# More engines for two early kinds of work, and an instruction order searched anew: attention in hash buckets with a two-layer network behind it

## The chip, the cores and the metric

The kernel runs on one core of one Trainium2 chip. TensorE (PE, with PEld for its weight loads) does the matrix products, VectorE (DVE), ScalarE (ACT) and GpSimd (POOL) the elementwise work, SyncE (SP) issues the transfers. Each engine works through its own instructions in the order in which they were written, and they wait for each other by semaphores. The metric is the time of one execution on the device in microseconds (us); less is better. Three executions of the kernel before took 867.09, 869.69 and 871.51 us.

## The reference

```python
# q, k, v: (4, 8, 768, 64), times 0.1; proj: (64, 6); w_in: (512, 2048); w_out: (2048, 512)
q_bits = (einsum('bhsd,dk->bhsk', q, proj) > 0);  k_bits = (einsum('bhsd,dk->bhsk', k, proj) > 0)
mask = bucket(q_bits)[:, :, :, None] == bucket(k_bits)[:, :, None, :]      # the six bits as a number
scores = where(mask, matmul(q, k^T) / sqrt(64), -1e9)
attn = exp(scores - max(scores));  attn = attn / (sum(attn) + 1e-9)
x = matmul(attn, v), its heads side by side: (3072, 512)
out = (maximum(x @ w_in, 0) ** 2) @ w_out                                   # (3072, 512)
```

## The kernel before

Work goes by visits: one batch, one pair of heads, one third of the 768 queries. Each visit has four units of 128 queries by 768 keys. A unit's scores go to a PSUM tile (`pS`, later also `side`), VectorE takes the row maxima (`line`), ScalarE the exponentials with their sums (`e`, `sm`), and `rv` becomes one over the sum. The attention is then transposed (`aT`) and multiplied by the values (`pA`); four visits give one block of 256 tokens, and `moe` runs the two layers on it (`pm` against `win`, `po` against `wo`), interleaved with the next visits.

The matrix products of most stages are made of float16 pairs, a high and a low part. Only the first visits are "plain": their scores are products in float32 with the mask's rows set into the same operands (`A`, `L`, `Q`, `M`; some rows of these are made on VectorE and ScalarE out of the PSUM tile `side`), and for the first four of them the division `e * rv` is written back to `e`, and TensorE transposes it against the unit matrix `unit_f` into `pT`. A visit that isn't plain divides into the pair `hl`, which a transfer transposes.

The weights come as 64-bit integers holding a double each. `fetch` loads a piece of 128 x 512 shifted by two bytes (`raw`, in `room`), has one 16-bit half of each number copied out ("the top half", `move(first...)`), and VectorE then joins it with the rest. There are 32 such pieces, 16 of each matrix; a norm of each group (`sq`, `norm`) and the split into a high and a low part follow.

Nothing of the order is written by hand. `Program` collects all operations with their dependences. Some name several engines that may do them ("ways"). A planner in the kernel's own code then lists them: `forward` takes, at each moment of its own clock, the ready operation of best priority on each engine, and chooses among ways by estimated end; `backward` and 24 `rounds` set the priorities; then each number in `PATH` stands for one pseudo-random shake of the priorities (`shake`), all kept, one after the other. The last `forward` is the order emitted. Estimated times decide on engines and order alone: on the chip every wait is a real semaphore.

Transfers are estimated so, one after another at `HBM` = 265 bytes a ns (265 GB/s), with a shorter time for those issued in the first `SOON_TO` ns:

```python
done *= SOON if t < SOON_TO else 1.0                       # forward and replay; SOON, SOON_TO = 0.7, 22000
dma = max(dma, t + busy + (650 if k != "pool" else 450))   # when this transfer may start
dma += done
done = dma + 910 - t                                       # when its data has landed
```

`emit` also fills TensorE's queue: where the plan has TensorE idle before the first transposition, it puts products of the constant `ones` (tile `idle`), in number after the planned gap:

```python
fill[i] = int((o.start - end) * IDLE_SHARE / 56) if fill else int((o.start - end) * 0.95 / 107)
```

with `IDLE_SHARE` = 0.6. The functions that the change touches:

Of the kernel before, what the change touches and what calls it, by code (L numbers as in the profile page):

```python
# [13 lines left out]
BF16 = mybir.dt.bfloat16  # L14
# [35 lines left out]

ROUNDS, BEHIND = 24, 40000
PATH = (
# [13 lines left out]
)  # L66
LOADS = 0

# [3 lines left out]

PLAIN, PLAIN_TO, ALTERNATE, DOUBLE = 4, 12, 16, 34

PLAIN_AV, DIVIDE = (0, 1, 2, 3), ("pool",)

AV_RUN = 18

# [15 lines left out]

SWITCH, ENTRY = 95, 105
TRANSPOSES, HBM, SMALL = 165, 265, 300
SOON, SOON_TO = 0.7, 22000


class Buffer:  # L100
# [477 lines left out]
def lsh_attention_moe(ctx: ExitStack, tc, kq, v, proj2, w_in, w_out, consts, out):  # L578
# [5 lines left out]
    pe, dve, act, pool, sp = pr.pe, pr.dve, pr.act, pr.pool, pr.sp  # L584
# [3 lines left out]
    def send(out, x):  # L588
        sp.dma_start(out, x)

    def move(out, x, scale=1.0, engines=(act, dve, pool)):
        ways = [(q, "tensor_scalar", (out, x, scale, 1.0, ALU.mult, ALU.mult), {}) for q in engines if q not in (act, sp)]
        if act in engines:
            ways.append((act, "activation", (out, x, AF.Identity if isinstance(scale, View) else AF.Copy), {"scale": scale}))
        if sp in engines:
            ways.append((sp, "dma_start", (out if out.dtype == x.dtype else out.bitcast(x.dtype), x), {}))
        pr.add(*ways)
# [67 lines left out]
    def fetch(src):  # L665

        raw = place(turn[0] % 2 * 4096, 4096, U32).rearrange("p (n t) -> p n t", t=2)
        send(raw.rearrange("p n t -> p (n t)").bitcast(U16)[:, 0:2047], src.bitcast(U16)[:, 1:2048])
        first = tops[turn[0] % len(tops)]
        turn[0] += 1  # L670
        move(first[:, :, 1], raw.rearrange("p n t -> p (n t)").bitcast(BF16).rearrange("p (n t) -> p n t", t=4)[:, :, 2], 1.0, (dve, pool))
        f = place(12288 + turned[0] % ((ROOM - 12288) // 2048) * 2048, 2048, F32)
        turned[0] += 1
        dve.scalar_tensor_tensor(f.bitcast(U32), raw[:, :, 0], 13, first.rearrange("p n t -> p (n t)").bitcast(U32), ALU.logical_shift_right, ALU.bitwise_or)
        return f
# [16 lines left out]
    def split(srcs, parts, name):  # L692

        fs = [fetch(src) for src in srcs]
        pt = small("pt")
        for n, f in enumerate(fs):
            sq = sb([P, 512], BF16, "sq", 2)
            square(sq, f)
            pe.matmul(pt, ones, sq, start=n == 0, stop=n == len(fs) - 1)
        norm = sb([P, 1], F32, "norm")  # L700
        dve.tensor_reduce(norm, pt, AX.X, ALU.max)
        to, back = scales(norm, name, 4)
        for f, (hi, lo) in zip(fs, parts):
            move(hi, f, to)
            left(lo, f, to, hi)
        return to, back
# [405 lines left out]
```

## Time and profile before

| | before |
|---|---|
| median of three executions | 869.69 us (867.09 to 871.51) |
| the profiled execution | 867.13 us |
| its span, first to last instruction | 865.1 us, 16,996 instructions |
| mean granted TensorE clock over the span | 0.996 of full speed |
| busy: TensorE, ScalarE, VectorE, GpSimd | 832.1, 666.0, 661.7, 111.5 us |

All rows and views are of the one profiled execution, so 867.13 - 865.1 = 2.03 us of its time lie outside the span. A matmul's row ends by a model and matmuls are pipelined, so busy time of TensorE includes short waits in its pipeline. Most operations are recorded by one helper line, L565, and are told apart by their tiles.

### The profile page before, as it was taken

Reading aid. Unit: us, or ns where it says so; the run is one execution under the profiler, and the core shown is the slowest. Engines: PE = TensorE matmul, PEld = TensorE weight load, DVE = VectorE, ACT = ScalarE, POOL = GpSimd, SP = SyncE. Lnnn points to the kernel's source line nnn. Section 1 sums busy time; section 2 is a strip of 40 time slices with the busy share of each in tenths; the row PEclk is TensorE's granted clock in tenths of the full one; section 3 lists DMA queues with packets and bytes.
Section 4 is the critical chain, followed back from the end, with each engine's and each line's share of the span. In section 5 each row is a group of like instructions: output and inputs, shape, how many; then the busy total and the mean of one; then the engine's idle time right before and its main releaser. Section 6 shows DMA issues by size and latency. Waiting matters only on the chain.

```text
span 865.1 us, 16996 instructions
## 1 busy us (share of the span) xinstructions
PE 832.1 (96%) x6340; PEld 543.8 (63%) x6343; DVE 661.7 (76%) x1448; ACT 666.0 (77%) x1153; POOL 111.5 (13%) x175
## 2 busy tenths in 40 slices
PE   6999978998999999999999999999999999999997
PEld 4555555665566667667666667676666666766664
DVE  4889988999696999877796888885887988871111
ACT  3897867699796888877886898977887888883332
POOL 0554464310010100000000001000100000000000
PEclk8999999999999999999999999999999999999999
DMA  8426979865788898787575978797665798771000
GB/s 298 128 82 185 195 197 226 188 117 108 177 168 189 159 166 163 143 156 169 134 156 153 165 155 146 151 159 164 135 111 157 145 150 150 135 147 38 1 25 25
DMA packets 301634, 125.77 MB, mean 145 GB/s; under 512 B 279792, under 2 KB 287728, under 8 KB 301552
## 3 DMA queue, kind: packets, MB, share of 16 engines
q1 hardware_dynamic: 301264, 124.61, 68.6%
q8 instruction: 50, 0.82, 0.4%
q14 instruction: 32, 0.26, 0.1%
q10 hardware_dynamic: 288, 0.08, 0.0%
HBM read 37.36 MB, written 6.29 MB: 50 GB/s over the span
## 4 chain that ended last, share of the span: by engine, by line
PE 73%; DVE 11%; ACT 8%; issue 3%; DMA 3%; POOL 1%; SPq 0%; ACTq 0%; DVEq 0%; POOLq 0%
PE pm L565 24%; PE po L565 24%; PE pA L558 9%; PE pS L565 8%; PE side L565 6%; DVE line L563 3%; ACT e L565 3%; DVE hl L565 2%; ACT g L565 1%; ACT hl L565 1%; PE pd L558 1%; DMA unit_f<-consts 1%; DMA V<-vp 1%; DVE room L565 1%; PE pc L565 1%
## 5 line engine op out<-in xcount | busy, mean ns | idle before, releaser
L565 PE MATMUL pm<-xx,win 128*128 128x256 f16 x2304 | 308.3, 273 | 3.0 <-DVE g L565 1.2
L565 PE MATMUL po<-wo,g 128*128 128x512 f16 x1152 | 298.7, 379 | 4.7 <-ACT acc L565 3.2
L565 PEld LDWEIGHTS <-win 128*128 128x128 f16 x2304 | 223.0, 98 | 84.0 <-issue 18.0
L565 DVE SCALAR_TENSOR_TENSOR hl<-e,rv,hl 128x768 f16<-128x768 f32 x176 | 179.5, 1025 | 15.8 <-ACT hl L565 14.8
L565 PEld LDWEIGHTS <-g 128*128 128x128 f16 x1152 | 111.4, 98 | 107.6 <-issue 11.2
L565 ACT ACTIVATE hl<-e,rv 128x768 f16<-128x768 f32 x168 | 155.2, 928 | 8.3 <-DVE rv L565 3.8
L563 DVE TENSOR_REDUCE line<-pS 128x1 f32<-128x768 f32 x113 | 107.8, 954 | 21.0 <-PE pS L565 18.9
L565 ACT ACTIVATE g<-g 128x512 f32<-128x512 f32 (+1 forms) x184 | 114.7, 625 | 10.3 <-PE po L565 7.7
L565 POOL TENSOR_SCALAR rv<-sm 128x1 f32<-128x1 f32 x98 | 37.9, 387 | 590.5 <-ACT e L565 558.3
L565 DVE SCALAR_TENSOR_TENSOR g<-g,g 128x512 f16<-128x512 f32 x84 | 57.7, 686 | 69.1 <-ACT g L565 69.0
L565 ACT ACTIVATE g<-pm 128x512 f32<-128x512 f32 x93 | 55.0, 591 | 68.6 <-PE pm L565 68.5
L558 PE MATMUL pA<-aT,VV 128*64 128x256 f16 x1584 | 94.9, 274 | 0.0
L558 PEld LDWEIGHTS <-VV 128*64 128x64 f16 x1584 | 83.1, 110 | 12.9 <-issue 12.5
L565 ACT ACTIVATE e<-pS,pair 128x768 f32<-128x768 f32 x72 | 71.0, 986 | 24.0 <-DVE pair L563 13.8
L565 ACT ACTIVATE e<-side,pair 128x768 f32<-128x768 f32 x72 | 71.0, 986 | 12.6 <-DVE pair L563 7.3
L563 DVE TENSOR_REDUCE line<-side 128x1 f32<-128x768 f32 x79 | 75.2, 951 | 5.0 <-PE side L565 4.0
L565 ACT ACTIVATE e<-pS,line 128x768 f32<-128x768 f32 x41 | 36.9, 899 | 8.3 <-DVE line L563 6.8
L565 PEld LDWEIGHTS <-room 128*128 128x128 f16 x288 | 27.8, 98 | 18.3 <-issue 1.3
L565 PE MATMUL pS<-A,L 128*128 128x384 f32 x84 | 34.9, 529 | 4.6 <-DVE L L565 2.4
L565 PE MATMUL pS<-room 128*128 128x384 f16 x144 | 36.0, 326 | 0.0
L565 PE MATMUL side<-room 128*128 128x384 f16 x144 | 34.6, 326 | 0.0
L565 PE MATMUL pS<-Q,M 128*128 128x384 f32 x80 | 31.3, 503 | 2.5 <-ACT e L565 2.3
(164 smaller groups left out, 905.6 us busy)
## 6 DMA issues: line engine op xcount, KB each, us to landing
R<-kq SPq DMA_DIRECT2D x24, 384.0 KB, 4.1
room<-w_in SPq DMA_DIRECT2D x16, 511.8 KB, 3.9
room<-w_out SPq DMA_DIRECT2D x16, 511.8 KB, 3.7
V<-vp SPq DMA_DIRECT2D x16, 384.0 KB, 4.1
out<-acc SPq DMA_DIRECT2D x24, 256.0 KB, 2.8
room<-room SPq DMA_DIRECT2D x60, 96.0 KB, 2.9
aT<-hl SPq DMA_TRANSPOSE x176, 3.9
Q<-kq SPq DMA_DIRECT2D x6, 384.0 KB, 4.1
```

The source lines that it names most:

```text
L558: ins = q.engine.matmul(*map(real, args), **kw).ins
L563: issue(q, getattr(q.engine, name)(*map(real, args), **{k: real(x) for k, x in kw.items()}).ins)
L565: ins = getattr(q.engine, o.name)(*map(real, o.args), **{k: real(x) for k, x in o.kw.items()}).ins
```

## The change

Two calls get more ways, the estimate of the first transfers loses its factor, and `PATH` holds another list: 233 shakes (400004 to 440621) give way to 3,588 (960005 to 1002083).

```diff
 PATH = (
-    400004, 400029, 400036, 400042, 400059, 400060, 400072, 400092, 400101, 400104, 400119, 400137, 400139, 400148, 400157, 400162, 400198, 400206,
...
+    960005, 960006, 960007, 960008, 960010, 960012, 960013, 960014, 960019, 960020, 960021, 960022, 960024, 960025, 960027, 960028, 960030, 960032,
...
-PLAIN_AV, DIVIDE = (0, 1, 2, 3), ("pool",)
+PLAIN_AV, DIVIDE = (0, 1, 2, 3), ("pool", "dve", "act")
...
-SOON, SOON_TO = 0.7, 22000
+SOON, SOON_TO = 1.0, 0
...
-        move(first[:, :, 1], raw.rearrange("p n t -> p (n t)").bitcast(BF16).rearrange("p (n t) -> p n t", t=4)[:, :, 2], 1.0, (dve, pool))
+        move(first[:, :, 1], raw.rearrange("p n t -> p (n t)").bitcast(BF16).rearrange("p (n t) -> p n t", t=4)[:, :, 2], 1.0, (dve, pool, act))
```

`DIVIDE` is used at one place, `move(e, e, rv, ...)` of a plain unit: 16 divisions of 128 x 768 numbers in float32. The call in `fetch` is the copy of the top halves: 32 of them, 128 x 512 numbers of 16 bits. With the new ways ScalarE may do either kind as an activation (a copy, or a multiplication by a value per row), and VectorE the divisions too. Which engine gets which is the planner's choice.

## Rows read from the trace of the kernel before

**Rows 1.** The page: busy time of each engine with its share of the span and its number of instructions.

```profile
PE 832.1 (96%) x6340; PEld 543.8 (63%) x6343; DVE 661.7 (76%) x1448; ACT 666.0 (77%) x1153; POOL 111.5 (13%) x175
```

**Rows 2.** Busy time by stretch (the windows view). Columns: stretch in us from the span's start, its length, busy us of each engine with its number of instructions, granted TensorE clock as a share of full speed, busy share of the DMA engines, GB/s.

```profile
10.00:20.00 10.00, 4.23 (x8) 2.17 (x9) 3.97 (x9) 3.63 (x8) 0.76 (x1) 0.74 0.85 322
20.00:60.00 40.00, 37.21 (x207) 21.17 (x209) 34.36 (x74) 35.79 (x73) 20.22 (x29) 0.98 0.34 109
60.00:110.00 50.00, 47.15 (x286) 27.91 (x285) 47.09 (x99) 39.84 (x75) 23.91 (x28) 1.00 0.81 185
110.00:150.00 40.00, 33.21 (x217) 20.15 (x218) 35.28 (x67) 30.04 (x53) 21.61 (x23) 1.00 0.85 203
150.00:200.00 50.00, 47.62 (x336) 30.08 (x334) 47.92 (x98) 41.60 (x70) 9.93 (x17) 1.00 0.81 167
200.00:600.00 400.00, 394.86 (x3169) 260.83 (x3169) 329.58 (x742) 332.33 (x570) 23.50 (x49) 1.00 0.79 157
600.00:850.00 250.00, 250.00 (x1988) 169.69 (x1988) 156.84 (x344) 175.20 (x300) 10.84 (x22) 1.00 0.54 105
```

**Rows 3.** The chain that ended last, followed through its first 32 us. Columns: start in us, us, what.

```profile
2.63 7.21 DMA V<-vp
...
9.87 7.42 DMA unit_f<-consts
...
17.32 0.23 DVE ident L565
...
18.17 0.56 DVE Q L565
```

**Rows 4.** VectorE's instructions in order of time, 0 to 20 us. Columns: start in us, us, engine, line, operation, out<-in with shapes, count, and in brackets the idle time before it and what ended it.

```profile
17.32 0.23 DVE L565 CAST ident<-unit_f 128x128 bf16<-128x128 f32 x1 [5.70 <-DMA unit_f<-consts]
...
18.76 0.96 DVE L563 TENSOR_REDUCE line<-pS 128x1 f32<-128x768 f32 x1
```

**Rows 5.** TensorE's matmuls in order of time, 0 to 32 us, same columns.

```profile
0.99 4.00 PE L554 MATMUL idle<-ones 128*128 128x128 bf16 x38 [0.99 <-POOL ones L565]
...
7.25 1.45 PE L554 MATMUL idle<-ones 128*128 128x128 bf16 x23
11.14 1.41 PE L565 MATMUL pS<-A,L 128*128 128x384 f32 x2 [2.45 <-DVE L L565]
...
12.67 1.49 PE L565 MATMUL pS<-A,L 128*128 128x384 f32 x2
18.78 0.48 PE L565 MATMUL side<-bits,sgn 128*128 128x384 bf16 x1 [4.62 <-DVE Q L565]
19.05 2.75 PE L565 MATMUL pS<-A,L 128*128 128x384 f32 x4
...
29.60 0.81 PE L565 MATMUL pS<-A,L 128*128 128x384 f32 x2
...
30.89 1.46 PE L565 MATMUL pS<-A,L 128*128 128x384 f32 x4
```

**Rows 6.** All engines in order of time, 0 to 32 us, same columns: the first transfer's issue, and the first users of some of the first transfers.

```profile
0.74 0.40 SPq L565 DMA_DIRECT2D Q<-kq  x1
...
3.81 0.56 DVE L565 TENSOR_SCALAR M<-Q 64x768 f32<-64x768 f32 x1 [1.26 <-DMA Q<-kq]
...
7.92 0.56 DVE L565 TENSOR_SCALAR L<-A 64x768 f32<-64x768 f32 x1 [2.32 <-DMA A<-kq]
...
8.93 0.56 DVE L565 TENSOR_SCALAR M<-Q 64x768 f32<-64x768 f32 x1 [0.46 <-DMA Q<-kq]
...
9.87 0.84 ACT L565 ACTIVATE sqv<-V 128x768 bf16<-128x768 f32 x1 [3.00 <-DMA V<-vp]
...
13.49 0.76 POOL L565 TENSOR_SCALAR room<-room 128x512 f16<-128x512 bf16 x1 [8.40 <-DMA room<-w_in]
```

**Rows 7.** Groups of instructions by form in the stretch 0 to 200 us, GpSimd, then VectorE, then ScalarE. Columns: line, engine, operation, out<-in with shapes and count | busy us, mean ns of one | idle time before them and what ended it.

```profile
L565 POOL TENSOR_SCALAR room<-room 128x512 f16<-128x512 bf16 x26 | 24.8, 963 | 14.2 <-DMA room<-w_in 10.6 <-DMA room<-w_out 2.9
L565 POOL TENSOR_SCALAR e<-e,rv 128x768 f32<-128x768 f32 x16 | 17.0, 1064 | 15.4 <-DVE rv L565 10.0 <-PE side L565 1.7 <-DVE fromwin L565 1.4
...
L565 DVE TENSOR_SCALAR room<-room 128x512 f16<-128x512 bf16 x6 | 2.9, 481 | 0.1
...
L565 DVE TENSOR_SCALAR hl<-e,rv 128x768 f16<-128x768 f32 x2 | 1.2, 612 | 0.0
...
L565 ACT ACTIVATE hl<-e,rv 128x768 f16<-128x768 f32 x25 | 23.2, 928 | 1.2 <-DVE rv L565 1.2
...
L565 ACT ACTIVATE g<-g 128x512 f16<-128x512 f32 x8 | 5.0, 628 | 4.2 <-PE po L565 4.1
```

**Rows 8.** GpSimd's instructions on the tiles e (the divisions) and room (the copies of the top halves, to 200 us), one row each. Columns: line, engine, operation, out<-in, count: shortest, median and longest ns, first and last start in us, form.

```profile
L565 POOL TENSOR_SCALAR e<-e,rv x16: 904/907/1323, 24.4 to 75.2; 128x768 f32<-128x768 f32 x16
...
L565 POOL TENSOR_SCALAR room<-room x26: 757/774/1513, 13.5 to 164.0; 128x512 f16<-128x512 bf16 x26
```

**Rows 9.** What TensorE waited for, 20 to 200 us and then 200 to 600 us. Columns: who waited <- for whom: us in total, times, the longest.

```profile
PE pS L565 <- ACT e L565: 4.2, 6, 1.7
PE side L565 <- DVE Q L565: 2.2, 5, 0.8
PE pT L565 <- ACT aT L565: 1.2, 2, 0.9
...
PE po L565 <- ACT acc L565: 3.2, 5, 0.8
```

212 rows, old and new, of the table PATH are left out of this document.

## The prediction

> **What bounds the kernel now.** Read the busy shares first: TensorE has work in 96% of the span, no other engine in more than 77% [rows 1]. A change to engines off TensorE's queue can so give back no more than the time in which TensorE waits, 865.1 - 832.1 = 33.0 us. The view by stretches says where that is [rows 2]. From 600 to 850 us TensorE is busy 250.00 of 250 us: nothing to win. From 200 to 600 us it is idle 5.1 us. From 20 to 200 us the busy times sum to 165.2 of 180 us, idle 14.8, the worst part being 110 to 150 us with 6.8. From 10 to 20 us it is busy 4.23 of 10 us, and the granted clock is 0.74, a mixture of the two levels of 2.4 and 1.2 GHz; from 60 us on it is 1.00. So the change must earn its time in the first 200 us, where it also acts: the divisions by GpSimd lie between 24.4 and 75.2 us, its copies of top halves between 13.5 and 164.0 us [rows 8].
>
> Next the chain of waits through the start [rows 3]. Two transfers head it: the first `V`, and then `unit_f`, issued at 9.87 and landed 7.42 us later, for a single VectorE cast (`ident`) at 17.32 us. VectorE had been idle 5.70 us ahead of that cast [rows 4], and what is queued behind it was ready long before: a pair of score products had started on TensorE at 11.14 us and run 1.41 us [rows 5], yet the row maximum of the first scores runs at 18.76 us [rows 4]. TensorE's next product, at 18.78 us, waits 4.62 us for the `Q` that VectorE makes at 18.17 us [rows 3, 5]. An in-order queue is thus held by a transfer whose result nothing needs so early.
>
> The stall has a second price. The score products around it run slow: pairs of 1.41 and 1.49 us and a run of four in 2.75 us, together 5.65 us; later a pair takes 0.81 and a run of four 1.46, so the same eight would take 3.08 us [rows 5]. That is 2.6 us at the lower clock after idle time.
>
> **The estimates of first transfers.** The planner's formulas can be held against the landings. For loads of 384 KB (393,216 bytes) one after another, with about 1.9 us ahead of the first (issue from 0.74 [rows 6], then 0.475 and 0.65 by the code) and 0.91 behind, the old estimate has 0.7 x 393,216 / 265 = 1.04 us each, landing at about 3.8, 4.9, 5.9, 7.0 and 8.0 us; the new one 1.48 us each, at 4.3, 5.8, 7.2, 8.7 and 10.2. The first users started at 3.81 (first), 7.92 and 8.93 (third and fourth) and 9.87 (fifth) [rows 6]. The old estimate is up to 2 us early, the new one within 0.7 us. Ahead of `unit_f` lie ten such loads and two of 512 KB, 4.98 MB in all: the old estimate lands it at about 1.9 + 13.2 + 0.2 + 0.9 = 16.2 us, the new one at 21.8, the trace at 17.29 [rows 3]. So the old plan put work behind transfers that came later than it believed; the new plan, if wrong, is wrong on the side where data waits for its user.
>
> **The change part by part.**
>
> *Start.* With the later estimate the planner has a reason to put the cast of `ident` behind the row maxima and the `Q` rows. From above: the whole TensorE wait of 4.6 us and the 2.6 us at the lower clock, 7.2 us. From below 0: the transfers keep the DMA engines 85% busy from 10 to 20 us [rows 2], and another late piece (a `V`, an integer piece of the weights) may stop the same queue. The cast's own wait is the nearest row and most of it has no need to be; against that VectorE is busy 34.4 of the next 40 us and ScalarE 35.8 [rows 2], so part of an earlier start is lost downstream. I take 4.0.
>
> *Filling products.* Longer planned gaps mean more products of `ones` in TensorE's queue. The first gap had 38, in 4.00 us [rows 5]: 105 ns each. The plan's landing of the second load moves by 0.9 us, which at 0.95 / 107 is 8 more, 0.8 us, and real work behind them waits if data is there first. On the other side filled gaps hold the clock up: after 23 of them, from 7.25 us, the next real product came at 11.14 [rows 5]. Bounds -2.6 (already in the 7.2 above) and +0.8; taken: +0.3.
>
> *Copies of top halves.* Now 26 on GpSimd of 963 ns and 6 on VectorE of 481 [rows 7]. ScalarE's price isn't in the trace; the nearest row is its conversion of 128 x 512, 628 ns [rows 7]. Each copy moved from GpSimd shortens one step by about 0.34 us and the longest, 1,513 ns [rows 8], by 0.9. But nobody on the path stands behind them much: GpSimd is busy 75.7 of 180 us from 20 to 200 us.
>
> *Divisions.* Now 16 on GpSimd of 1,064 ns. Nearest rows: the same sizes, but with a 16-bit result, on VectorE 612 ns and on ScalarE 928 [rows 7]. A division moved is 0.14 to 0.45 us shorter, on the path from the exponential to the transposition. Yet TensorE's waits at the transpositions name ScalarE's `aT` (1.2 us) [rows 9], the copy after them. Both kinds together: gain 0 to 2, taken 0.5. What hides their new cost is ScalarE's idle time: 180 - 147.3 = 32.7 us from 20 to 200 us [rows 2]. All 42 from GpSimd would cost 26 x 0.628 + 16 x 0.928 = 31.2 us, all of that cover; about a third of them, 10 us, fits. The waits 20 to 200 us show what happens without cover: the largest, 4.2 us, are on ScalarE's exponentials [rows 9], which would stand behind a copy in the same queue.
>
> GpSimd's shortest copy takes 757 ns, its longest 1,513, and the division 904 to 1,323 [rows 8]: something holds it at times. The Trainium skill (SBUF — State Buffer, section "SBUF: two separate sides") says that VectorE and GpSimd share one pair of ports, which one of them locks for a whole instruction; the spread agrees with it. It also speaks against the new way on VectorE: a VectorE division would lock out GpSimd. By that rule alone the sum would lose, at 0.612 us each for 16, at most 9.8 us of GpSimd's time, which is idle for more than half of this stretch, and so nothing at the end.
>
> *The order from 20 to 200 us.* All of it is new. From above 14.8 us, TensorE's whole idle time; from below the same amount lost, since nothing in the trace says how a different order falls. What speaks for a gain: 110 to 150 us has 17% idle where 60 to 110 us has 5.7% with VectorE fuller (47.1 of 50 against 35.3 of 40) [rows 2], so an order that packs 110 to 150 us alike would save 6.8 - 2.3 = 4.5 us. I take a third, 1.5.
>
> *After 200 us.* 5.1 us idle in 400, of which 3.2 us are waits for `acc` [rows 2, 9]; the rest of TensorE's work is the same. Bounds -4 and +3, taken -0.3.
>
> Sum: -4.0 + 0.3 - 0.5 - 1.5 - 0.3 = -6.0 us. The profiled execution goes from 867.1 to 861.1 us. The median of the three runs is 869.69, 2.6 us above that execution, so the forecast of the median is 863.7 us.
>
> **Rivals.**
>
> *A, the start's gain doesn't last.* The stall at 17 us goes, or changes into one for another transfer, and the gain is eaten: VectorE is busy 92% and ScalarE 82% from 20 to 200 us [rows 2], a chain that needs each of them per unit. For it: that fullness, and DMA engines 85% busy in the stalled stretch. Against: VectorE itself was stopped at 17 us. Time: 1 us for the start, 0.5 for the rest: 868.2, between 865.5 and 873. That the new ways stay unused would cost only their 0.5 us: 864.2, within the forecast.
>
> *B, slower: ScalarE becomes the bound.* Copies and divisions stand in ScalarE's queue ahead of exponentials. It decides from the point where more than the 32.7 us of its idle time, or most of it, is filled: at all 42 operations, 31.2 us, ScalarE has 1.5 us left of 180, and if a third of the 31.2 shows as waits of TensorE that is 10.4 us. With 4.0 won at the start and nothing else, 869.7 + 10.4 - 4.0 = 876 us, between 873 and 882. For it: the largest waits of TensorE are ScalarE's already. Against: the planner weighs ScalarE's estimated end in each choice. The Trainium skill (ScalarE: Activation LUTs, section "Rules for kernel authors") would have multiplications on VectorE and not on ScalarE; by the rows here, 612 against 928 ns, the sum for 16 divisions would differ by 5.1 us of engine time, not of path.
>
> *C, much better.* The new order takes the 7.2 us of the start and over half of the 14.8 us, 8: 869.7 - 15.7 (with 0.5 for the new ways) = 854 us.
>
> **How the numbers follow.** One half per cent of 869.7, 4.35 us, is about what a measurement of this kernel can tell from no change: under 865.3 is faster, over 874.0 slower. Chances: forecast 0.50 (857 to 867; 0.43 of it under 865.3), A 0.25 (none of it under 865.3), B 0.15 (a little of it, 0.01, under 874.0), C 0.10. Faster 0.43 + 0.10 = 0.53; same 0.07 + 0.25 + 0.01 = 0.33; slower 0.14. The range leaves out the better half of C and the worse half of B with some of its rest, 0.15 in all: 853 to 876.
>
> **What the profile after would show.** Right: no VectorE idle time of some 5 us ahead of the cast of `ident`; TensorE's busy time from 10 to 20 us well over 4.23 us with a clock over 0.74; TensorE idle from 20 to 200 us below 14.8 us; ScalarE rows for `room` copies or for `e<-e,rv`, some 10 to 20 together. Wrong: a like stall on another transfer (A), ScalarE over 165 of 180 us with TensorE waiting for `e` far more than 4.2 us (B), more than 46 filling products ahead of the first real one, or TensorE losing time after 200 us, where the order is as new as elsewhere.

## The result, and the profile after

The changed kernel takes 874.91 us (median of 13 executions, 871.39 to 876.41); the kernel before 868.87 us (13 executions, 867.06 to 871.51). The ratio is 1.0064 [1.0053, 1.0076]: 6.0 us slower, where the prediction had 6.0 us faster. The time lies inside the predicted range, on its wrong side.

The profiled execution took 873.61 us with a span of 871.5 us, 6.4 more than before. The page, the line that answers to [rows 1]:

```profile
PE 831.8 (95%) x6338; PEld 543.8 (62%) x6338; DVE 662.0 (76%) x1451; ACT 671.4 (77%) x1162; POOL 98.2 (11%) x163
```

TensorE works as long as before (831.8 against 832.1), so all of the loss is TensorE waiting: 871.5 - 831.8 = 39.7 us, before 33.0. The view by stretches, columns as in [rows 2]:

```profile
10.00:20.00 10.00, 4.18 (x22) 1.91 (x21) 3.24 (x7) 1.76 (x4) 0.96 (x2) 0.87 0.85 339
20.00:60.00 40.00, 36.55 (x182) 20.07 (x182) 34.54 (x78) 35.90 (x72) 12.90 (x21) 0.90 0.31 89
60.00:110.00 50.00, 42.00 (x257) 24.98 (x255) 45.10 (x91) 43.65 (x80) 18.83 (x26) 1.00 0.76 187
110.00:150.00 40.00, 34.75 (x236) 21.79 (x234) 37.71 (x72) 32.10 (x57) 18.07 (x20) 1.00 0.95 207
150.00:200.00 50.00, 49.51 (x349) 31.60 (x347) 46.63 (x94) 42.13 (x74) 20.66 (x20) 1.00 0.78 162
200.00:600.00 400.00, 392.72 (x3160) 260.32 (x3160) 328.30 (x742) 329.94 (x564) 20.04 (x54) 1.00 0.78 156
600.00:850.00 250.00, 247.68 (x1963) 167.10 (x1960) 158.92 (x350) 175.68 (x300) 5.69 (x16) 1.00 0.56 108
```

Taking TensorE's column from that of [rows 2]: 0.05 us lost from 10 to 20, 0.66 from 20 to 60, 5.15 from 60 to 110, 2.14 from 200 to 600 and 2.32 from 600 to 850; 1.54 and 1.89 won from 110 to 150 and 150 to 200. Together 6.9 us lost. 110 to 150 us, which the prediction wanted packed, did get better, but 60 to 110 us got worse by three times as much, and the last third, which had been full, now has gaps.

The start, all engines in order of time, columns as in [rows 4]:

```profile
0.99 4.08 PE L742 MATMUL idle<-ones 128*128 128x128 bf16 x46 [0.99 <-POOL ones L753]
5.00 0.52 PE L746 MATMUL side<-A,pj 128*32 128x384 f32 x2
...
9.22 0.33 SPq L753 DMA_DIRECT2D unit_f<-consts  x1
...
17.17 0.23 DVE L753 CAST ident<-unit_f 128x128 bf16<-128x128 f32 x1 [6.70 <-DMA unit_f<-consts]
...
18.63 0.90 ACT L753 ACTIVATE e<-pS,line 128x768 f32<-128x768 f32 x1 [7.55 <-DVE line L751]
...
19.68 2.93 PE L753 MATMUL pS<-Q,M 128*128 128x384 f32 x4 [5.82 <-ACT e L753]
...
25.61 0.81 PE L753 MATMUL pS<-A,L 128*128 128x384 f32 x2
```

The stall that was to go is still there. VectorE stands idle 6.70 us ahead of the same cast, and TensorE 5.82 us, 1.2 more than its 4.62 of [rows 5]; `unit_f` landed some 7.9 us after its issue.

The new ways were used. Groups by form from 0 to 200 us, columns as in [rows 7]:

```profile
L753 POOL TENSOR_SCALAR room<-room 128x512 f16<-128x512 bf16 x11 | 10.6, 967 | 10.8 <-DMA room<-w_in 7.7 <-DVE hl L753 1.6 <-DMA room<-w_out 1.2
L753 POOL TENSOR_SCALAR e<-e,rv 128x768 f32<-128x768 f32 x9 | 8.2, 909 | 7.1 <-DVE rv L753 7.0
...
L753 DVE TENSOR_SCALAR e<-e,rv 128x768 f32<-128x768 f32 x4 | 2.5, 616 | 0.1
L753 DVE TENSOR_SCALAR room<-room 128x512 f16<-128x512 bf16 x4 | 2.2, 538 | 0.0
...
L753 ACT ACTIVATE room<-room 128x512 f16<-128x512 bf16 x17 | 13.3, 780 | 0.7 <-DMA room<-w_in 0.7
L753 ACT ACTIVATE e<-e,rv 128x768 f32<-128x768 f32 x3 | 2.8, 926 | 0.0
```

ScalarE has 20 of the 48 operations, 16.1 us. TensorE's largest wait from 20 to 200 us (columns as in [rows 9]):

```profile
PE pS L753 <- ACT e L753: 14.8, 9, 5.8
```

The waits on ScalarE's exponentials rose from 4.2 to 14.8 us [rows 9]. Of these 5.8 are the stall at the start, whose product begins at 19.68 us and runs on past 20; the kernel before has its stall of 4.62 us ahead of 20 us, outside this count. From 24 to 200 us the kernel before still has its 4.2 us, and the kernel after:

```profile
PE pS L753 <- ACT e L753: 8.9, 8, 2.2
```

A reading lies near: the new work on ScalarE holds up the exponentials, as the rival B said. The experiments show that it is wrong.

### The profile page after: what moved, and what is told of

The parts are those of the page before. It is cut to its first block, busy times and chain, and to the rows that moved or that the text cites. A ratio compares the mean times of both kernels' runs of the same rounds, so it can differ in the third digit from the quotient of the medians.

```text
span 871.5 us, 16958 instructions
## 1 busy us (share of the span) xinstructions
PE 831.8 (95%) x6338; PEld 543.8 (62%) x6338; DVE 662.0 (76%) x1451; ACT 671.4 (77%) x1162; POOL 98.2 (11%) x163
## 5 line engine op out<-in xcount | busy, mean ns | idle before, releaser
L753 PE MATMUL po<-wo,g 128*128 128x512 f16 x1152 | 302.1, 379 | 6.3 <-ACT acc L753 4.4
L753 ACT ACTIVATE g<-g 128x512 f16<-128x512 f32 (+1 forms) x183 | 113.1, 626 | 10.5 <-PE po L753 7.9
L753 POOL TENSOR_SCALAR rv<-sm 128x1 f32<-128x1 f32 x93 | 30.5, 328 | 536.1 <-ACT e L753 535.3
L753 PE MATMUL pS<-A,L 128*128 128x384 f32 x84 | 33.1, 505 | 2.6 <-ACT e L753 2.5
```

Source lines behind the costliest of these rows:

```text
L753: ins = getattr(q.engine, o.name)(*map(real, o.args), **{k: real(x) for k, x in o.kw.items()}).ins
```

## The experiments

The theories were: that the stall behind the cast costs what the prediction said, but wasn't removed; that the new ways cost (B); that the longer estimate of the first transfers makes a worse order; that the 3,588 shakes do. All times are medians, all ratios to the kernel before on the same chip, where its medians are 869.1 to 869.5 us. "The plan" is what the kernel's own planner reckons for the order that it emits.

**The cast put behind what needs no `unit_f`.** In both kernels one operation is taken out of the finished order and put in just ahead of its first user. Nothing else of the order moves.

```diff
         out = self.order()
+        cast = next(i for i in out if self.ops[i].name == "tensor_copy")
+        user = next(i for i in out if cast in self.ops[i].deps)
+        out.remove(cast)
+        out.insert(out.index(user), cast)
```

> The changed kernel with one instruction moved: VectorE's cast of ident goes to just ahead of its first user (about 29 us in the plan), nothing else in any queue changes. Theory S (the start: the stall of VectorE behind unit_f was left in place, 6.70 us of idle time at 17.17 us in the changed kernel's trace, and it is worth what I had put on it): 869 to 872 us instead of 874.9, the stall gone or under 2 us. Rival P (the stall is eaten downstream, where VectorE and ScalarE are 86 to 90% busy from 20 to 60 us): 874 to 876 us, with the idle time turning up on VectorE or TensorE before 60 us.

> The kernel before with the same move of the cast of ident (5.70 us of idle time ahead of it). Theory S: 864 to 866 us instead of 868.9, about as much won as in the changed kernel, so that this beats both. Rival P: 868 to 870 us.

The kernel after with it takes 869.52 us, 1.0004 [0.9991, 1.0016]: 5.4 less than the kernel after. The kernel before with it takes 862.91, 0.9926 [0.9910, 0.9942]: 6.2 less, and faster than both kernels. VectorE's instructions in order of time, kernel before with this edit:

```profile
23.55 0.55 DVE L569 TENSOR_SCALAR Q<-side 64x384 f32<-64x384 f32 x1 [0.41 <-PE side L569]
24.14 0.23 DVE L569 CAST ident<-unit_f 128x128 bf16<-128x128 f32 x1
24.28 0.16 DVE L569 RECIPROCAL rv<-rv 128x1 f32<-128x1 f32 x1
```

The cast now runs at 24.14 us with no idle time ahead of it. So the stall had about the price that the prediction gave it, and the change left it where it was. Part of that price is TensorE's clock. The median of the mean granted clock over the executions is 0.995 for the kernel before and 0.999 with the cast moved, 0.994 and 0.997 for the kernel after. What the clock falls short of 1, times the span, is the time that it costs if TensorE is busy all the while: 4.3 and 0.9 us, 5.2 and 2.6 (the clock is on record in steps of 0.9 us). So at most 3.4 of the 6.2 and 2.6 of the 5.4 us are the clock; the rest is waiting. The 6.0 us that the change lost are to be found even without it (862.9 against 869.5).

**The new work given back to GpSimd.** The order of the kernel after is kept; every copy of a top half that it gives to ScalarE, and every division not on GpSimd, is issued on GpSimd at the same place of the order. `given` holds the 32 copies and 16 divisions.

```diff
         out = self.order()
+        for i in self.given:
+            o = self.ops[i]
+            if o.queue is self.act or len(o.ways) == 3 and o.ways[0][0] is self.pool:
+                o.queue, o.name, o.args, o.kw = next(w for w in o.ways if w[0] is self.pool)[:4]
```

> The changed kernel's order with the new ways undone in place: the 17 copies of top halves and 3 divisions on ScalarE and the 4 divisions on VectorE go to GpSimd, each at its place in the list; every other instruction stays where it was. Theory E (ScalarE's 16.1 us of new work delays the exponentials: TensorE waits 4.2 us for them from 60 to 110 us, where before it waited about 1.3): 870 to 872 us. Rival O (the order is to blame, and built around the engines it chose): 875 to 885 us, since GpSimd's copies take 0.96 us where ScalarE's take 0.78.

880.35 us, 1.0134 [1.0108, 1.0160]: 5.4 us slower than the kernel after. Its groups by form from 0 to 200 us, GpSimd's:

```profile
L757 POOL TENSOR_SCALAR room<-room 128x512 f16<-128x512 bf16 x28 | 26.0, 934 | 11.0 <-DMA room<-w_in 7.6 <-DMA room<-w_out 2.4 <-DVE norm L757 0.3
L757 POOL TENSOR_SCALAR e<-e,rv 128x768 f32<-128x768 f32 x16 | 15.2, 949 | 9.5 <-DVE rv L757 7.0 <-DVE tov L757 2.2
```

VectorE's joins of the pieces of the weights in it (columns as in [rows 8]; the number ahead of the semicolon is the start of the last join):

```profile
L757 DVE SCALAR_TENSOR_TENSOR room<-room x32: 673/684/1666, 17.0 to 170.6; 128x512 uint32<-128x512 uint32 x32
```

And the same joins in the kernel after:

```profile
L753 DVE SCALAR_TENSOR_TENSOR room<-room x32: 674/685/1241, 18.5 to 168.0; 128x512 uint32<-128x512 uint32 x32
```

And the waits for exponentials in it, from 24 to 200 us:

```profile
PE pS L757 <- ACT e L757: 7.8, 5, 2.3
```

With the work back on GpSimd these waits fall from 8.9 to 7.8 us, and yet the kernel is slower. The last piece of the weights is joined 2.6 us later, and the granted clock is lower, 0.989 (median of six executions) against 0.994, at most 9.7 us lost by it against 5.2. B is refuted as the account of the loss: work taken off ScalarE doesn't win the time back. This order was made for the new ways, so the 5.4 us are what they are worth in it, not in another.

**No shakes.** In both kernels the list is emptied.

```diff
 PATH = (
-    960005, 960006, 960007, 960008, 960010, 960012, 960013, 960014, 960019, 960020, 960021, 960022, 960024, 960025, 960027, 960028, 960030, 960032,
...
 )
```

> The changed kernel with an empty list of shakes: its other three edits, and the order that the rounds alone give. The plan reckons this order 7.7 us longer than the shaken one. Theory F (the chip follows the plan): 881 to 884 us. Rival O (at this scale the chip does not follow the plan; what the shakes win on paper is lost to stalls that the plan does not see): 870 to 878 us.

> The kernel before with an empty list of shakes; the plan reckons it 6.4 us longer than the shaken order (853.7 against 847.3 us). Theory N (the chip does not follow the plan within some 8 us, orders scatter around 870 to 875 whatever the settings): 868 to 876 us, so that the before's list too has won little, and the changed kernel's settings, 872.9 us without shakes, have cost little. Theory V (the old settings make the better order, and the loss comes from the settings): 866 to 870 us. Theory F (the chip follows the plan from these settings): 875 to 877 us.

The kernel after without shakes takes 872.88 us, 1.0044 [1.0028, 1.0060]: 2.0 less than with its 3,588. The kernel before without its 233 takes 868.88, 0.9996 [0.9985, 1.0006]: no different. In the plan the shakes win 7.7 us (853.7 to 846.0) and 6.4 (853.7 to 847.3). The unshaken kernel before has only 2.97 us of idle time ahead of its cast, so that its 233 shakes won something elsewhere and made the stall longer; the pair with the cast moved, below, separates the two.

**Either edit alone, and part of the shakes.** The unshaken kernel before gets the longer estimate (the first pair of lines), the unshaken kernel after gets the old one back (the same pair the other way round), and the kernel after keeps its first 1,200 shakes.

```diff
-SOON, SOON_TO = 0.7, 22000
+SOON, SOON_TO = 1.0, 0
...
-        for seed in PATH:
+        for seed in PATH[:1200]:
```

> No shakes, the old ways, and of the change only the longer estimate of the first transfers (SOON = 1.0, SOON_TO = 0). The plan reckons 857.5 us, 3.7 more than with the old estimate, most of that in transfers that it believes slower. Theory V, if the estimate costs: 3 to 5 us slower than the kernel before without shakes. Theory N: within 3 us of it.

> No shakes, the old estimate of transfers, and of the change only the new ways. The plan reckons 850.1 us, 3.7 less than with the old ways. Theory E (ScalarE's new work costs): 2 to 5 us slower than the kernel before without shakes. Theory G (the new ways help, as giving them back in the changed order has lost 5.4 us): 2 to 5 us faster than it. Theory N: within 3 us.

> The changed kernel with the first 1,200 of its 3,588 shakes; the plan reckons 847.7 us, against 853.7 without shakes and 846.0 with all. Theory F: between 872.9 us (none) and something clearly under it, so 867 to 869 us. Theory N: anywhere from 868 to 878 us, with no order between none (872.9), these, and all (874.9).

The longer estimate alone: 878.08 us, 1.0103 [1.0087, 1.0119]. The new ways alone: 861.23 us, 0.9906 [0.9891, 0.9921], faster than both kernels, and with ScalarE doing even more of the work: 22 copies and 5 divisions. The first 1,200 shakes: 873.15, 1.0046 [1.0032, 1.0060], nothing won against none, though the plan fell from 853.7 to 847.7.

So two edits of one change pull against each other. Where the two kernels differ (in both edits), the stretches from 20 to 200 and from 200 to 300 us show, columns as in [rows 2]. The kernel with the new ways alone:

```profile
20.00:200.00 180.00, 166.54 (x1055) 102.61 (x1058) 166.29 (x342) 155.99 (x281) 72.84 (x88) 0.98 0.73 170
200.00:300.00 100.00, 96.45 (x725) 61.09 (x725) 80.10 (x196) 81.11 (x142) 6.18 (x14) 1.00 0.75 157
```

The kernel with the longer estimate alone:

```profile
20.00:200.00 180.00, 161.85 (x975) 97.93 (x977) 161.03 (x332) 138.38 (x256) 68.99 (x87) 0.97 0.66 158
200.00:300.00 100.00, 91.69 (x705) 57.87 (x705) 78.19 (x183) 80.64 (x134) 12.10 (x17) 1.00 0.69 155
```

TensorE is 4.7 us fuller from 20 to 200 us and 4.8 us fuller from 200 to 300, 9.5 of the 16.9 us between the two. ScalarE is fuller too, by 17.6 us: work there isn't what holds TensorE. The joins with the new ways alone:

```profile
L551 DVE SCALAR_TENSOR_TENSOR room<-room x32: 672/683/1152, 19.8 to 162.1; 128x512 uint32<-128x512 uint32 x32
```

The joins with the longer estimate alone:

```profile
L551 DVE SCALAR_TENSOR_TENSOR room<-room x32: 664/682/1571, 18.2 to 172.8; 128x512 uint32<-128x512 uint32 x32
```

The last piece of the weights is joined 10.7 us earlier with the new ways alone.

**Other draws.** A change of an estimate redraws the whole order, so one pair doesn't tell an effect from luck. With the new ways and no shakes: the factor 0.75 (the first pair of lines), likewise 0.85, and, to draw anew without touching the factor, 22 rounds in place of 24 (the second pair) with 1.0 and with 0.7.

```diff
-SOON, SOON_TO = 1.0, 0
+SOON, SOON_TO = 0.75, 22000
...
-ROUNDS, BEHIND = 24, 40000
+ROUNDS, BEHIND = 22, 40000
```

> New ways, no shakes, estimate factor 0.75 (plan 846.5 us). Theory X (the longer the first transfers are believed to be, the slower the chip; 861.2 us at 0.7, 872.9 at 1.0): 861 to 864 us. Theory D (each setting only draws another order; the estimate as such is worth little): anything from 857 to 873 us, without order in the factor.

> New ways, no shakes, factor 0.85 (plan 847.8 us). Theory X: 865 to 868 us, between 0.7 and 1.0. Theory D: 857 to 873 us, as likely under the 0.75 run as over it.

> New ways, no shakes, factor 1.0 as in the change, but 22 rounds instead of 24, so that another round's order is kept (plan 855.9 us against 853.7). Theory X: 872 to 876 us, like the first order of this setting. Theory D: a few us away from 872.9, most likely below (862 to 871 us), since that one was a poor draw.

> New ways, no shakes, factor 0.7 as before, 22 rounds, another round's order (plan 851.7 us against 850.1). Theory X: 860 to 864 us, like the first order of this setting. Theory D: most likely above 861.2 us (863 to 872 us), since that one was a good draw.

0.75: 862.90 us, 0.9925 [0.9906, 0.9944]. 0.85: 865.76, 0.9960 [0.9945, 0.9974]. 1.0 with 22 rounds: 877.88, 1.0099 [1.0071, 1.0127]. 0.7 with 22 rounds: 869.94, 1.0003 [0.9990, 1.0017]. Shorter estimates are faster again, in the order of the factor as theory X said, but two fewer rounds alone move the time by 8.7 us (861.2 to 869.9) and by 5.0 (872.9 to 877.9), the latter past what either theory expected.

**The estimate in the priorities or in the listing.** The rounds set the priorities, and a last `forward` lists the order. New ways, no shakes; priorities found with 0.7 and the last listing with 1.0 (shown), and the other way round. `best[3]` and `best[4]` are the priorities of the best round.

```diff
-        self.restore(best[2])
-        return best[1]
+        global SOON, SOON_TO
+        SOON, SOON_TO = 1.0, 0
+        return self.forward(best[3], best[4])
```

> New ways, no shakes; the priorities of the rounds with the factor 0.7 (861.2 us as listed with 0.7), but the last listing made with 1.0. The plan reckons it 856.9 us with its own estimate. Theory X (the longer estimate by itself makes a slower order): 870 to 876 us. Theory D (it only draws another order): anything in 860 to 878 us, near what other orders of a like plan measured.

> New ways, no shakes; the priorities of the rounds with the factor 1.0 (872.9 us as listed with 1.0), the last listing made with 0.7. The plan reckons it 857.3 us, 3.6 more than with 1.0. Theory X: 864 to 870 us, faster than 872.9 although its plan is longer. Theory D: 868 to 880 us, not faster than 872.9.

The same priorities listed with 1.0 in place of 0.7: 871.55 us, 1.0021 [1.0012, 1.0030], 10.3 more than 861.23. Listed with 0.7 in place of 1.0: 870.12, 1.0003 [0.9992, 1.0015], 2.8 less than 872.88. The sign is the same, the size is not.

**The account without the stall.** The four lines that move the cast, in the unshaken kernel after, in the unshaken kernel with the new ways alone, in the unshaken kernel before and in the unshaken kernel with the longer estimate alone.

> The changed kernel without shakes (872.9 us) with the cast of ident moved to its first user. Reading W (the shakes won on paper only: 7.7 us in the plan, nothing on the chip, also where VectorE isn't stopped at the start): 866 to 869 us, not above the shaken order with the same move (869.5). Reading S2 (the shaken order was only hit harder by the start's stall): 871 to 874 us, so that with the stall away the shakes are worth 2 us or more.

> New ways, old estimate of transfers, no shakes (861.2 us), with the cast of ident moved to its first user. If the stall is a price of its own, the same in each order: 854.5 to 857 us, as 5.4 and 6.2 us were won in the two shaken orders. If this order had slack to take the stall up: 859 to 862 us.

> The kernel before without shakes (868.9 us, with only 2.97 us of idle time ahead of the cast of ident), the cast moved to its first user. If the stall's price goes with its length: 865 to 867 us, so that the before's shakes are worth 2 to 4 us once the stall is out of both (862.9 shaken). If those shakes too were worth nothing: 861 to 864 us.

> Old ways, the longer estimate, no shakes (878.1 us), the cast moved to its first user: the last cell of the table of four without the stall, beside before_unshaken_cast, ways_cast (857.6) and unshaken_cast (867.3). If the longer estimate costs as much without the stall as with it (9.2 and 11.7 us): 871 to 876 us, 7 us or more over before_unshaken_cast. If what it cost was a longer stall: 864 to 868 us.

| medians, us | stall left in | cast moved |
|---|---|---|
| kernel before | 868.87 | 862.91 |
| its shakes away | 868.88 | 867.36, 0.9978 [0.9964, 0.9992] |
| then the new ways | 861.23 | 857.64, 0.9854 [0.9834, 0.9874] |
| then the longer estimate | 872.88 | 867.28, 0.9976 [0.9960, 0.9992] |
| then the 3,588 shakes: kernel after | 874.91 | 869.52 |
| old ways with the longer estimate, no shakes | 878.08 | 871.20, 1.0018 [1.0007, 1.0029] |

Read down the right column: the old shakes were worth 4.5 us; the new ways win 9.7; the longer estimate takes 9.6 back; the new shakes lose 2.2. In all 4.5 - 9.7 + 9.6 + 2.2 = 6.6 us lost, with the stall left in 6.0. What the longer estimate costs is partly a longer stall. With the old ways it costs 9.2 us with the stall left in (868.88 to 878.08) and 3.8 without it (867.36 to 871.20), with the new ways 11.7 and 9.6. So of the two expectations of the last run neither holds in full: the time is within 871 to 876 us, but not 7 us over the unshaken kernel before. VectorE's cast in that kernel, one execution:

```profile
12.15 0.23 DVE L551 CAST ident<-unit_f 128x128 bf16<-128x128 f32 x1 [2.97 <-DMA unit_f<-consts]
```

And with the longer estimate alone:

```profile
16.87 0.23 DVE L551 CAST ident<-unit_f 128x128 bf16<-128x128 f32 x1 [6.07 <-DMA unit_f<-consts]
```

857.64 us is the fastest kernel of this study, 1.5% under the kernel before. Two of its stretches:

```profile
10.00:20.00 10.00, 7.51 (x52) 4.08 (x50) 7.18 (x13) 6.56 (x14) 1.56 (x3) 1.00 0.97 359
...
60.00:110.00 50.00, 46.97 (x297) 28.71 (x296) 47.70 (x100) 43.95 (x81) 18.93 (x26) 1.00 0.85 192
```

TensorE is busy 7.51 us from 10 to 20 us with a granted clock of 1.00, where the kernel after has 4.18 and 0.87; and 46.97 from 60 to 110, where that has 42.00.

**Where the new shakes lose.** The pair with the cast moved (869.52 and 867.28 us). The page's busy time, and the stretches from 200 to 600 and from 600 to 850 us. With all 3,588 shakes, span 868.5 us:

```profile
PE 833.3 (96%) x6338; PEld 543.8 (63%) x6338; DVE 662.3 (76%) x1451; ACT 671.1 (77%) x1162; POOL 96.5 (11%) x163
...
200.00:600.00 400.00, 393.71 (x3182) 260.70 (x3181) 325.40 (x737) 327.78 (x565) 19.97 (x53) 1.00 0.78 156
600.00:850.00 250.00, 247.15 (x1935) 165.99 (x1933) 158.62 (x349) 174.99 (x298) 5.67 (x16) 1.00 0.54 105
```

TensorE's largest wait from 600 to 850 us:

```profile
PE po L757 <- ACT acc L757: 2.1, 3, 0.8
```

With none, span 863.7 us:

```profile
PE 828.3 (96%) x6335; PEld 542.8 (63%) x6338; DVE 665.3 (77%) x1454; ACT 672.9 (78%) x1157; POOL 88.1 (10%) x165
...
200.00:600.00 400.00, 391.48 (x3170) 258.44 (x3168) 325.42 (x733) 334.65 (x574) 19.26 (x56) 1.00 0.78 158
600.00:850.00 250.00, 249.98 (x1956) 168.85 (x1955) 157.28 (x343) 172.64 (x295) 13.72 (x23) 1.00 0.53 104
```

From 600 to 850 us the shaken order loses 2.8 us of TensorE's busy time, 2.1 of them three waits of up to 0.8 us for the copy of a sum out of PSUM to `acc` on ScalarE. The same three stand in the kernel after, and none in the kernel before. But from 200 to 600 us it wins 2.2, and over the whole span TensorE waits as long in both: 868.5 - 833.3 = 35.2 us and 863.7 - 828.3 = 35.4. What differs is its busy time, by 5.0 us for the same products, and busy time includes short waits in TensorE's pipeline. So where the new shakes lose their 2.2 us isn't shown.

**What stays open.** Four unshaken orders listed with 1.0 took 871.6, 872.9, 877.9 and 878.1 us, mean 875.1; six with 0.7 to 0.85 took 861.2, 862.9, 865.8, 868.9, 869.9 and 870.1, mean 866.5. The medians don't overlap, though the nearest lie 1.4 us apart, and TensorE's busy time from 60 to 110 us tells nearly the same: 41.4 to 44.8 in the six profiles listed with 1.0 (the kernel after and its 1,200 shakes among them), 44.0 to 47.2 in the seven listed with less. That the longer estimate costs is well supported. That it costs 9.6 us is not: draws within one setting differ by 5 to 9. The same holds for the new ways, whose gain came out as 3.9, 5.2, 5.4, 7.7 and 9.7 us in the five comparisons above, with one redrawn order (869.94) that has none. TensorE's clock is part of these differences too, reckoned as for the cast: at most 3.4 us are lost by it with the new ways alone, 7.0 when the longer estimate is added, so up to 3.6 of those 11.7 us; 7.8 with 22 rounds at 0.7, up to 4.4 of that redraw's 8.7. Why an order planned for late data is worse was not settled: the longer stall and the clock are parts of it, and no single wait accounts for the rest.

## Why the prediction was wrong

**The start.** The failed step is "With the later estimate the planner has a reason to put the cast of `ident` behind the row maxima and the `Q` rows." Right behind the three lines of the planner's code that were quoted stands another rule, for small transfers:

```python
if o.ways[0][4][1] < SMALL:
    dma, done = at0, busy + 2200
```

`SMALL` is 300 ns; `unit_f` is 65,536 bytes, 65,536 / 265 = 247 ns. The planner has it land 2.2 us after its issue, whatever is queued, in both kernels; `SOON` never touches that. The prediction worked out landings of 16.2 and 21.8 us for it by the rule for large transfers; the plan had 9.4, so the planner saw no stall to move the cast away from. The stall stayed, 6.70 us. The price was sound: 4.0 us taken within 0 to 7.2, and the runs give 6.2 (kernel before) and 5.4 (after), of which the clock is up to 3.4 and 2.6 where the prediction had 2.6 of its 7.2.

**The longer estimate.** "The new plan, if wrong, is wrong on the side where data waits for its user" was read as harmless, and no cost entered the sum. The estimate is indeed nearer to the landings [rows 6], and still it lost in each of the seven comparisons, 2.8 to 11.7 us. A term for it was missing from the sum; by what mechanism it costs stays open, beyond the longer stall and the clock.

**The new ways.** Right in kind and in use (20 operations on ScalarE; "some 10 to 20" was said), but a gain of 0.5 within 0 to 2 was taken where five comparisons show 3.9 to 9.7 and one redrawn order none. The step "nobody on the path stands behind them much" looked at GpSimd's busy share. Behind each copy stands a join, behind the joins the weights, and the copies on GpSimd had stretched to 1,513 ns [rows 8]; with the new ways alone the last join comes at 162.1 us, before at 164.8, without shakes at 167.0. That the joins are what the gain comes from fits these numbers, but no run changes them alone.

**Filling products.** Eight more, 46, as worked out, but in 4.08 us against 4.00: 89 ns each, not 105. The first real product came earlier than before (5.00 us against 5.38), so the 0.8 us was not lost: +0.3 taken, about 0 true. That filled gaps hold the clock up isn't borne out by the row named for it: after those 23 products and 2.45 us of idle time the pair at 11.14 us took 1.41 us [rows 5], as slow as those after the stall.

**The order.** From 20 to 200 us -1.5 was taken and +2.4 came; after 200 us -0.3, and 2.1 + 2.3 = +4.5 came, past the bound of +3. This was one of the signs named ("TensorE losing time after 200 us"). The shakes were treated as part of "the order" without a sign of their own; they won 7.7 us on paper and lost 2 on the chip.

**The rivals.** A, that the start's gain is eaten, doesn't fit: there was none. B gave nearly the time (876) by a mechanism that two experiments refute. No rival said that the estimate itself could make the order worse, though the text noted that all of the order is new. So that the time fell within the range, near B's, was luck. The chance of slower, 0.14, was too low for a change in which every instruction is placed anew.

## What to carry to other kernels

When a planner's estimate is to move an operation, read every branch that sets that operation's time, down to its size class; a profile that shows the stall doesn't show that the edit reaches it, and moving the one operation by hand gave 5 to 6 us for four lines. Time the parts of a joint change apart: here a good one (more engines for a slowed kind of work) was hidden by a loss of like size, and a more accurate estimate went with slower orders. Microseconds won by a long search on a model are not yet time: 7.7 in the plan were a loss of 2, and among unshaken orders two redraws lay 5 to 9 us apart, so compare several draws before giving one a cause.

## What the runs showed of the hardware

ScalarE's copy of the top halves, 128 x 512 of 16 bits, took 780 ns (759 to 802 over 17), not the 628 ns of the conversion of the same size in [rows 7]. The Trainium skill (ScalarE: Activation LUTs, section "What ACT_TABLE_LOAD costs") gives 186 ns and 0.833 ns per element for an activation with immediate scale and bias, by which 512 elements would take 613 ns. The conversion agrees with that; the copy, which reads every fourth 16-bit number and writes every second, doesn't, and which of these costs isn't shown. VectorE did the same copy in 538 ns on the mean, GpSimd in 967, and giving it and the divisions back to GpSimd cost time, so even at 780 ScalarE was the better place here. A transfer of 64 KB issued at 9.2 to 9.9 us behind some 5 MB of others landed 7.4 to 7.9 us later in both kernels, where the plan has 2.2. Idle time cost twice here too: the score products right after the stall took 2.93 us for four, a pair at 25.61 us 0.81; the granted clock was 0.90 over 20 to 60 us in the kernel after (0.98 in the kernel before, whose lower clock fell mostly ahead of 20 us) and 1.00 in the fastest kernel, whose VectorE doesn't stand idle for the cast.
